# Two buffers for gathered token rows, and one slot's preparation moved by one place

## The chip, the cores and the metric

The kernel runs on one core of a Trainium2 chip. The metric is the device time of one execution in microseconds (us), taken over several runs. The engines of the core are TensorE (PE in the profile; PEld is its weight load), VectorE (DVE), ScalarE (ACT), GpSimd (POOL) and SyncE (SP), which here only issues DMAs.

## The reference

Banded attention is followed by a mixture of experts with one expert per token.

```python
# attention: 8 batches, 8 heads, 576 positions, 64 columns a head
mask_plain = (rel >= 0) & (rel < 32)                       # heads 0-3
mask_dil = (rel >= 0) & (rel < 128) & (rel % 4 == 0)       # heads 4-7
scores = np.where(masks, (q @ k.T) / 8, -1e9)
attn = softmax(scores);  x = (attn @ v) as [4608, 512]
# experts: 8, with 512 -> 1024 -> 512
logits = x @ w_gate + modality_bias[modality_id]
e_idx = argmax(logits);  gate_w = softmax(logits)[e_idx]
for e in range(8):
    mask = e_idx == e
    out[mask] = gate_w[mask, None] * (relu(x[mask] @ w1[e]) @ w2[e])
```

All inputs and outputs are float32.

## The kernel before

**Attention.** The work is cut into 72 units (9 for each batch). In the main loop (L1160) each turn does one stage of several units: `scores` (L420: products of q and k, the mask added by DVE, the row maximum, and the subtraction `sm` on POOL), `exp` on ACT, `probsT`, `attend`, `normalize`, and then the store of x into DRAM (`x_dram`, two halves) and the gate's logits. Products into `pss` (one buffer) for the next unit can start when DVE has read the last ones.

**Constants.** The generator `constants` (L239) is advanced beside the first turns. It sets up tables for the routing: POOL sets the buffer `xr` to zero (L251), fills `sent`, and makes index ramps (`pay`, `place`, `ewt_i`, `eoff_i`); DVE turns these into float tables (L281 to L294). DVE's instructions stand in the order of the code, so that its steps for the constants stand ahead of the mask addition of the unit that follows.

**Routing.** `gating` (L556) works out each token's expert and its place in a table in DRAM, and writes the tokens' numbers there by scatters from POOL (L619, six a batch). Groups of 256 tokens of one expert are called slots. The first four slots are taken after three batches, so that the experts' work can begin before attention has ended. There are 19 slots in the static part (the last holds 128 tokens), numbered from 0; "the third slot" is slot 2.

**A slot's rows.** The rows take this way:
- `fetch_ids` (L757): SP loads the token numbers `idt` of the slot.
- `gather` (L766): POOL fetches the rows with four indirect DMAs into the SBUF buffer `xr` (L775); SP writes `xr` to `x_slot` in DRAM (L780), and, when the slot before has been read (`taken`), loads it back as `xg` in another layout with four DMAs (L786). `xr` has one buffer, which one memset in `constants` has set to zero, since a row whose number is out of bounds is not written.
- `prepare_x` (L926): for each half of 128 tokens DVE transposes blocks of `xg` into `xt` (L937), ACT casts `xt` to the rounded part `xh` (L943), and DVE subtracts for the rest `xl` (L946). The four steps are: transpose of half 0; cast and subtraction of half 0; transpose of half 1; cast and subtraction of half 1.

**A slot's products.** `slots` (L971) does for each slot eight columns of work, f = 0 to 7, called places here. At each place PE makes twelve products of w1 and x into `ph` (L1071): for each of four blocks of rows `w1h * xh`, `w1h * xl` and `w1l * xh`. Then ACT and DVE make `hh` and `hl` (L1077, L1078) from the result, and PE makes the six second products (L989) of an earlier place. After them stand `split_w2` of this place and `split_w1` for the place after the next one; a split is a cast on ACT (L955) and a subtraction on DVE (L956). At the end of a slot ACT scales the result into `ys` (L992) and POOL scatters it to the output.

**What sets the order.** `ahead(n, f, end)` (L1096) is called twice at each place of slot n. It asks for weight loads, token numbers and gathers of later slots, one step a call. At the end of a place (`end`) it also does one step of `prepare_x` for slot n + 1, from a place on that the condition in L1116 gives. PE, DVE, ACT and SP keep the order of the code; POOL's order is set when the program is built, but most of its instructions (those by way of `pool`, among them gathers, memsets, output scatters) keep the order of the code among themselves. Each engine works through its queue in order, SP's DMA issues included.

Of the kernel before, what the change touches and what calls it, by code (L numbers as in the profile page):

```python
# [10 lines left out]
F32 = mybir.dt.float32  # L11
# [13 lines left out]
DM = H * D  # L25
# [33 lines left out]
def kernel(  # L59
# [13 lines left out]
    P = 128  # L73
# [4 lines left out]
    gat = ctx.enter_context(tc.tile_pool(name="gat", bufs=2))  # L78
# [160 lines left out]
    def constants():  # L239

        yield
        nc.scalar.copy(out=wgs[:, :, 0:NE], in_=wg)
        yield
        mid_t = spare[1][0:B, 0:S]
        for i in range(2):
            for a in range(2):
                nc.vector.tensor_copy(out=mid_t.rearrange("b (a c i j) -> b a i c j", a=2, c=2, i=2)[:, a, i],
                                      in_=mid[i][:, :, 0].rearrange("b (j c a) -> b a c j", c=2, a=2)[:, a])
            yield
        yield  # L250
        pool.memset(gat.tile([P, 2, DM], F32, name="xr", bufs=1), 0.0)  # L251
        sent = spare[1][:, S:S + (NE + 1) * NT * 3 // P].bitcast(I32)
        pool.memset(sent, SENT)
        yield
        pm = psum['o'].tile([P, 512], F32, name="po")
        for c in range(NGB):
            nc.tensor.transpose(out=pm[0:GB, B * c:B * (c + 1)], in_=mid_t[:, GB * c:GB * (c + 1)], identity=ident[:B, :B])
        mid_f = cpool.tile([GB, NBLK], F32, name="mid_f")
        nc.vector.tensor_copy(out=mid_f.rearrange("p (b c) -> p c b", c=NGB), in_=pm[0:GB, 0:NBLK].rearrange("p (c b) -> p c b", b=B))
        yield  # L260
        mid_n = cpool.tile([GB, NBLK], F32, name="mid_n")
        nc.vector.tensor_scalar(out=mid_n, in0=mid_f, scalar1=-1.0, scalar2=1.0, op0=ALU.mult, op1=ALU.add)
        mtmp = cpool.tile([GB, NE, NBLK], F32, name="mtmp")
        nc.gpsimd.tensor_tensor(out=mterm, in0=mid_n.rearrange("p (o c) -> p o c", o=1).broadcast_to([GB, NE, NBLK]),
                                in1=bias_sb[:, 0, :].rearrange("p (e o) -> p e o", o=1).broadcast_to([GB, NE, NBLK]), op=ALU.mult)
        nc.gpsimd.tensor_tensor(out=mtmp, in0=mid_f.rearrange("p (o c) -> p o c", o=1).broadcast_to([GB, NE, NBLK]),
                                in1=bias_sb[:, 1, :].rearrange("p (e o) -> p e o", o=1).broadcast_to([GB, NE, NBLK]), op=ALU.mult)
        nc.gpsimd.tensor_tensor(out=mterm, in0=mterm, in1=mtmp, op=ALU.add)
        yield
        nc.sync.dma_start(out=table.rearrange("(p a) t -> p (a t)", p=P), in_=sent)  # L270

        pool.iota(pay[:, :, 2], pattern=[[GB, NBLK]], base=0, channel_multiplier=1)
        place = cpool.tile([GB, 2, NBLK], I32, name="place")
        pool.iota(place[:, 0], pattern=[[0, B], [GB, NGB]], base=0, channel_multiplier=1)
        pool.iota(place[:, 1], pattern=[[S, B], [0, NGB]], base=0, channel_multiplier=0)
        ewt_i = cpool.tile([GB, NE, NGB], I32, name="ewt_i")
        pool.iota(ewt_i, pattern=[[-1, NE], [0, NGB]], base=NE, channel_multiplier=0)
        eoff_i = cpool.tile([GB, NE, NGB], I32, name="eoff_i")
        pool.iota(eoff_i, pattern=[[NT, NE], [0, NGB]], base=0, channel_multiplier=0)
        yield  # L280
        nc.vector.tensor_copy(out=ewt, in_=ewt_i)  # L281
        nc.vector.tensor_copy(out=eoff, in_=eoff_i)
        pool.memset(ones_bf, 1.0)
        pool.affine_select(out=upper, in_=ones_bf, pattern=[[1, GB]], compare_op=ALU.is_gt,
                                fill=0.0, base=0, channel_multiplier=-1)
        for t in x_dram:
            nc.sync.dma_start(out=t[NT:NT + 1, :], in_=zero)
        placef = cpool.tile([GB, 2, NBLK], F32, name="placef")
        nc.vector.tensor_copy(out=placef, in_=place)
        past = cpool.tile([GB, NBLK], F32, name="past")  # L290
        nc.vector.tensor_scalar(out=placef[:, 1], in0=placef[:, 0], scalar1=float(NCLS), scalar2=None, op0=ALU.mult)
        for r in range(1, NCLS):
            nc.vector.tensor_scalar(out=past, in0=placef[:, 0], scalar1=float(CL * r), scalar2=float(NCLS * CL - (2, -1, 2)[r - 1]), op0=ALU.is_ge, op1=ALU.mult)
            nc.vector.tensor_tensor(out=placef[:, 1], in0=placef[:, 1], in1=past, op=ALU.subtract)  # L294
        yield
        nc.vector.tensor_copy(out=place[:, 0], in_=placef[:, 1])
        nc.vector.tensor_tensor(out=pay[:, :, 0], in0=place[:, 0], in1=place[:, 1], op=ALU.add)
        yield
        nc.vector.tensor_copy(out=sidx[:, :, 0], in_=sidx_i)
# [22 lines left out]
    pool = InOrder()  # L322
# [443 lines left out]
    def gather(n, ids):  # L766


        idt, nu = ids
        xr = gat.tile([P, 2, DM], F32, name="xr", bufs=1)  # L770
        nrows = round_rows(n)
        queue = nc.sync
        for u in range(nu):
            for kd in range(2):
                pool.indirect_dma_start(out=xr[:, u, 256 * kd:256 * kd + 256], out_offset=None, in_=x_dram[kd][0:nrows, :],  # L775
                                        in_offset=bass.IndirectOffsetOnAxis(ap=idt[:, u, 2 * kd:2 * kd + 1], axis=0),
                                        bounds_check=nrows - 1, oob_is_err=False)
                yield
        yield
        queue.dma_start(out=x_slot[0:P * nu, :].rearrange("(u p) c -> p u c", p=P), in_=xr[:, 0:nu])  # L780
        yield
        while 0 < n < NS and n - 1 not in taken:
            yield
        xg = gat.tile([P, 2 * KC, P], F32, name="xg", bufs=1)
        for r in range(KC):
            queue.dma_start(out=xg[BLK * r:BLK * (r + 1), 0:nu * KC],  # L786
                              in_=x_slot[0:P * nu, P * r:P * (r + 1)].rearrange("(g i) c -> i g c", i=BLK))
        state['xg', n] = xg
# [30 lines left out]
    def round_rows(n):  # L819

        for (b, _), r0 in zip(EARLY, round_from[1:]):
            if n < r0:
                return (b + 1) * S
        return NT + 1
# [15 lines left out]
    def load_more(n, pieces):  # L840

        if n not in loads_of and n in si_of:
            loads_of[n] = [fetch_weights(si_of[n], n == 0), 0]
        if n in loads_of:
            for _ in range(min(pieces, 6 - loads_of[n][1])):
                next(loads_of[n][0], None)
                loads_of[n][1] += 1
# [119 lines left out]
    def split_w2(g):  # L967
        f = g % FC
        w2p[g] = split(w2q[f // 2][:, f % 2, :], [P, DM], "w2")

    def slots(ns, ids_of, ahead, hold=lambda n, f: (), base=0):  # L971


# [122 lines left out]
    def ahead(n, f, end):  # L1096

        if not end:
            todo['calls'] += 1
            load_more(n, 2)  # L1100
            i = todo['ids']
            if i < NS and i <= n + 3 and fetch_slot(i):
                todo['ids'] += 1
                born[i] = todo['calls']
            i = todo['rows']
            if not fetching and i < NS and i <= n + 2 and i in ids_of and todo['calls'] > born.get(i, -2) + 1:
                fetching.append((i, gather(i, ids_of[i])))
                todo['rows'] += 1
        if fetching and (not end or fetching[0][0] <= n + 1):
            if next(fetching[0][1], fetching) is fetching:  # L1110
                fetching.pop(0)
        if n + 1 == NS or not end or n + 1 not in ids_of:
            return
        due = sum(f >= x for x in (1, 2, 3, 5, 6, 7))
        load_more(n + 1, min(2, due - (loads_of[n + 1][1] if n + 1 in loads_of else 0)))
        if f >= (3 if n + 1 < 4 else 2):  # L1116
            if n + 1 not in preparing:
                preparing[n + 1] = prepare_x(n + 1, ids_of[n + 1])
            next(preparing[n + 1], None)
# [7 lines left out]

    units, turned = [], []
    tasks = [(-1, constants())]
    moe = None  # L1130
    man = ExitStack()
# [109 lines left out]
    with tc.For_i(NSTAT, NSTAT + left, 1) as i:  # L1241
        si = slot_regs(state['info', len(EARLY)], i)
        ids = fetch_ids(si)
        run(gather(NS, ids), fetch_weights(si, False), prepare_x(NS, ids), slots(1, [ids], lambda n, f, end: None, base=NS))
# [29 lines left out]
```

## Time and profile before

| | |
|---|---|
| median of 3 runs | 672.0 us (671.12 to 672.9) |
| profiled execution | 671.78 us |
| its span, first to last instruction | 670.0 us |
| mean granted TensorE clock | 0.989 |
| POOL's gathers (`xr<-x_dram`) | 74, median 1056 ns each |
| memset of `xr` | 1, 961 ns |
| transposes of `prepare_x` (L937) | 37, median 705 ns |

A row of a timeline reads: start, duration, engine, line, operation, output<-inputs, shapes, count, and in brackets the idle time of the engine before it with what ended that. A row of waits reads: who waited, for whom, us in total, times, the longest. "issue" is a wait for nothing that the profile shows. A granted clock of 1.00 is TensorE's full speed.

### The profile page before, as it was taken

The numbers are of one execution on the slowest core, as the hardware profiler recorded it, in microseconds if no ns is written. First come the engines' busy times: TensorE is split into PE (matmuls) and PEld (weight loads), VectorE is DVE, ScalarE is ACT, GpSimd is POOL, SyncE is SP. The second block draws the span as 40 slices with busy tenths as digits, with TensorE's granted clock in tenths as the row PEclk, the third lists the DMA queues.
The fourth block names the chain that finished last, engine by engine and source line by source line (L and its number), as shares of the span: only waits on it lengthen the run. The fifth ranks groups of instructions, "written<-read, shape, count | busy, mean of one in ns | idle before, by whom it ended". The sixth has DMA issues, their size and how long they took to land. (4 is left out here: it accounts for less than half of the span.)

```text
span 670.0 us, 17986 instructions
## 1 busy us (share of the span) xinstructions
PE 639.5 (95%) x6394; PEld 553.0 (83%) x6396; DVE 487.9 (73%) x1204; ACT 418.6 (62%) x897; POOL 258.6 (39%) x322
## 2 busy tenths in 40 slices
PE   8899999999998979999999999999999999999994
PEld 4788788778776868799989999899999999999972
DVE  6788888887789547977587668667776777677653
ACT  4677877877776345556566656665666566656663
POOL 5634665657766425333332232232413231321101
PEclk9999999999999789999999999999999999999998
DMA  9989899879879624976952338723312335931470
GB/s 196 222 203 213 188 195 211 156 181 203 194 164 246 181 45 99 230 167 181 256 172 72 88 95 258 183 80 111 123 68 79 111 117 128 274 97 64 109 185 24
DMA packets 133408, 103.33 MB, mean 154 GB/s; under 512 B 67424, under 2 KB 111474, under 8 KB 133316
## 3 DMA queue, kind: packets, MB, share of 16 engines
q1 hardware_dynamic: 124724, 82.30, 51.9%
q0 software_dynamic: 8176, 19.26, 9.8%
q8 instruction: 51, 0.84, 0.6%
q10 hardware_dynamic: 416, 0.59, 0.3%
q14 instruction: 41, 0.34, 0.2%
HBM read 127.52 MB, written 29.39 MB: 234 GB/s over the span
## 5 line engine op out<-in xcount | busy, mean ns | idle before, releaser
L1071 PE MATMUL pt<-xh,w1l 128*128 128x256 f32 x576 | 163.7, 284 | 2.1 <-DVE w1l L956 1.1
L1071 PE MATMUL pt<-xh,w1h 128*128 128x256 f32 x576 | 164.7, 286 | 0.9 <-issue 0.9
L1071 PE MATMUL pt<-xl,w1h 128*128 128x256 f32 x576 | 163.2, 283 | 1.6 <-DVE xl L946 1.6
L1077 ACT ACTIVATE hh<-pt 128x256 fp32r<-128x256 f32 x144 | 55.2, 383 | 151.8 <-PE pt L1071 144.1
L956 DVE TENSOR_TENSOR w2l<-w2q,w2h 128x512 fp32r<-128x512 f32 x152 | 104.5, 689 | 38.8 <-ACT w2h L955 24.8
L314 POOL DMA_INDIRECT xr<-x_dram,idt x74 | 82.2, 1111 | 112.6 <-DMA x_slot<-xr 69.0
L1071 PEld LDWEIGHTS pt<-xh,w1h 128*128 128x128 f32 x576 | 109.9, 191 | 9.4 <-issue 3.0
L314 POOL DMA_INDIRECT out_dram<-ys,idt x37 | 41.5, 1121 | 197.0 <-ACT ys L992 124.4
L1078 DVE SCALAR_TENSOR_TENSOR hl<-pt,hh 128x256 fp32r<-128x256 f32 x144 | 60.6, 421 | 76.4 <-ACT hh L1077 66.4
L1071 PEld LDWEIGHTS pt<-xl,w1h 128*128 128x128 f32 x576 | 109.8, 191 | 7.5 <-DVE xl L946 1.9
L989 PE MATMUL py<-w2h,hh 128*128 128x512 f32 x288 | 115.3, 400 | 0.0
L989 PE MATMUL py<-w2h,hl 128*128 128x512 f32 x288 | 114.0, 396 | 0.0
L989 PE MATMUL py<-w2l,hh 128*128 128x512 f32 x288 | 112.6, 391 | 0.0
L1071 PEld LDWEIGHTS pt<-xh,w1l 128*128 128x128 f32 x576 | 110.2, 191 | 2.4 <-DVE w1l L956 1.8
L956 DVE TENSOR_TENSOR w1l<-w1q,w1h 128x512 fp32r<-128x512 f32 x152 | 103.7, 684 | 6.4 <-ACT w1h L955 3.4
L955 ACT CAST w1h<-w1q 128x512 fp32r<-128x512 f32 x152 | 94.2, 622 | 5.9 <-PE py L989 3.1
L955 ACT CAST w2h<-w2q 128x512 fp32r<-128x512 f32 x152 | 93.0, 613 | 0.4 <-PE py L989 0.4
L314 POOL TENSOR_TENSOR sm<-sm,nmx 128x384 f32<-128x384 f32 x72 | 65.1, 904 | 71.8 <-DVE den L459 40.6
L445 ACT COPY pT<-pt 96x512 f32<-96x512 f32 x72 | 41.6, 578 | 46.4 <-PE pt L442 24.8
L989 PEld LDWEIGHTS py<-w2l,hh 128*128 128x128 f32 x288 | 54.4, 189 | 13.4
L452 PE MATMUL po<-vw,pT 96*64 96x65 f32 (+1 forms) x1216 | 54.0, 227 | 8.9 <-issue 3.1
L989 PEld LDWEIGHTS py<-w2h,hh 128*128 128x128 f32 x288 | 54.9, 191 | 6.9
(196 smaller groups left out, 1018.5 us busy)
## 6 DMA issues: line engine op xcount, KB each, us to landing
w2q<-in_moe_w_dram SPq DMA_DIRECT2D x76, 512.0 KB
w1q<-in_moe_w_dram SPq DMA_DIRECT2D x152, 256.0 KB
x_slot<-xr SPq DMA_DIRECT2D x18, 512.0 KB
xg<-x_slot SPq DMA_DIRECT2D x72, 128.0 KB
x_dram<-x_sb SPq DMA_DIRECT2D x32, 256.0 KB
st<-in_q_dram SPq DMA_DIRECT2D x32, 144.0 KB
st<-in_k_dram SPq DMA_DIRECT2D x32, 144.0 KB
vw<-in_v_dram SPq DMA_DIRECT2D x16, 288.0 KB
```

The costliest lines, as they stand in the source:

```text
L314: ins = tc.keep_in_program_order(getattr(nc.gpsimd, name)(*args, **kw))
L445: nc.scalar.copy(out=self.pT, in_=src)
L452: nc.tensor.matmul(out=pov[r0:r0 + nr, g, cs], lhsT=self.pT[:, 2 * g + a, r0:r0 + nr], rhs=self.vts[kd][:, blk, cs], start=True, stop=True)
L955: nc.scalar.copy(out=hi, in_=raw)
L956: nc.vector.tensor_tensor(out=lo, in0=raw, in1=hi.bitcast(F32), op=ALU.subtract)
L989: nc.tensor.matmul(out=py[u], lhsT=ht[:, us], rhs=wt, start=(f + n == 0), stop=(f + n == FC + 1))
L1071: nc.tensor.matmul(out=ph, lhsT=wt[:, c, :], rhs=xt[:, c, 0:cols], start=(c + i == 0), stop=(c + i == KC + 1))
L1077: nc.scalar.activation(out=hh, in_=ph, func=AF.Relu)
L1078: nc.vector.scalar_tensor_tensor(out=hl, in0=ph, scalar=0.0, in1=hh.bitcast(F32), op0=ALU.max, op1=ALU.subtract)
```

## The change

Three edits. `constants` sets two buffers to zero, with a second memset of the same size on POOL. `gather` takes its `xr` from two buffers in turn, so that a gather waits only for the x_slot write of the slot before the last one. And the condition for `prepare_x` gives place 3 as the first for slots 1 and 3 alone; slot 2 begins at place 2 of slot 1, as the slots from 4 on did already.

```diff
-        pool.memset(gat.tile([P, 2, DM], F32, name="xr", bufs=1), 0.0)
+        for _ in range(2):
+            pool.memset(gat.tile([P, 2, DM], F32, name="xr", bufs=2), 0.0)
...
-        xr = gat.tile([P, 2, DM], F32, name="xr", bufs=1)
+        xr = gat.tile([P, 2, DM], F32, name="xr", bufs=2)
...
-        if f >= (3 if n + 1 < 4 else 2):
+        if f >= (3 if n + 1 in (1, 3) else 2):
```

## The prediction

> **What bounds the kernel now.** I read the page first, then the busy time of the engines by stretches, then the waits of POOL and PE, and last the timelines of PE, DVE, POOL and SP around the places that the edits touch. The page:
>
> ```profile
> span 670.0 us, 17986 instructions
> PE 639.5 (95%) x6394; PEld 553.0 (83%) x6396; DVE 487.9 (73%) x1204; ACT 418.6 (62%) x897; POOL 258.6 (39%) x322
> ```
>
> TensorE is busy for 95% and POOL, whose waits the first edit is about, for 39%. An average over three stages says little, so here are seven stretches of the same execution (bounds, length, then busy time and count for PE, PEld, DVE, ACT, POOL, then granted clock, DMA share, GB/s):
>
> ```profile
> 0.00:30.00 30.00, 25.02 (x322) 16.93 (x325) 20.46 (x70) 16.89 (x39) 18.23 (x49) 1.00 1.09 198
> 30.00:215.00 185.00, 178.63 (x3275) 148.18 (x3274) 155.41 (x523) 141.07 (x324) 109.60 (x153) 1.00 0.89 197
> 227.00:241.00 14.00, 10.46 (x99) 8.10 (x98) 5.00 (x16) 4.53 (x10) 10.15 (x10) 1.00 0.48 95
> 241.00:246.00 5.00, 4.48 (x16) 2.98 (x16) 3.22 (x9) 2.14 (x5) 0.00 (x0) 0.66 0.13 43
> 256.00:262.00 6.00, 6.00 (x44) 5.46 (x43) 5.20 (x16) 2.58 (x6) 5.08 (x4) 1.00 0.43 114
> 262.00:290.00 28.00, 26.40 (x171) 23.48 (x171) 22.93 (x78) 16.73 (x35) 11.36 (x10) 1.00 0.93 194
> 290.00:650.00 360.00, 359.44 (x2280) 324.01 (x2278) 252.80 (x444) 215.81 (x444) 98.22 (x90) 1.00 0.48 137
> ```
>
> From 290 to 650 us, most of the mixture of experts, PE lacks only 360.00 - 359.44 = 0.56 us. Nothing that shortens a wait of another engine there can give more than that. What PE can still win lies before 290: 28.00 - 26.40 = 1.60 us between 262 and 290, and 3.54 + 0.52 = 4.06 us between 227 and 246, where the granted clock of the last 5 us is 0.66 as well.
>
> **The two gather buffers, at POOL.** The wait that they remove, and where it is longest:
>
> ```profile
> POOL xr L314 <- DMA x_slot<-xr: 69.0, 13, 15.3
> ...
> 227.06 1.46 POOL L314 DMA_INDIRECT xr<-x_dram,idt  x1 [6.28 <-DMA x_slot<-xr]
> 229.59 0.95 POOL L619 DMA_INDIRECT table<-pay,dst  x1 [1.07 <-DVE pay L610]
> ...
> 239.80 0.92 POOL L619 DMA_INDIRECT table<-pay,dst  x1 [0.30 <-issue]
> 256.01 1.47 POOL L314 DMA_INDIRECT xr<-x_dram,idt  x1 [15.29 <-DMA x_slot<-xr]
> ```
>
> ```profile
> 252.40 0.38 SPq L780 DMA_DIRECT2D x_slot<-xr  x1
> ```
>
> Thirteen gathers start late by 69.0 us in all, because the write of the rows to x_slot still reads the only buffer. With two, the first gather of slot 2 can start 6.28 us sooner, near 220.8, and slot 3's four 15.29 us sooner, near 240.7. Who gains from that? After the gather comes the x_slot write, on SP's queue. For slot 2 it was issued at 252.40, 11.7 us after POOL's block with its gathers had ended (239.80 + 0.92), so it waited for its turn on SP and not for the rows. Behind POOL's waiting gathers stand table scatters, whose inputs come from DVE (the one at 229.59 waits for pay), and the out scatters, which wait for ACT. I find no step of PE that waits for a gather, directly or through SP: I cost the removed wait at 0. The cover for that is PE's own work, and if it were gone, at most the 0.56 us of the late stretch and the 4.06 us of 227 to 246 could move; the second is a rival below. What is moved past: on POOL the gathers overtake nothing in the order of the code, only time; on SP no order changes.
>
> **The second memset.** It costs one more memset of the size of this one, on POOL, in the opening:
>
> ```profile
> 16.81 0.96 POOL L314 MEMSET xr<- 128x1024 f32 x1
> 17.70 0.92 POOL L314 MEMSET w1q<- 128x972 int32 x1
> ...
> 19.96 0.83 POOL L266 TENSOR_TENSOR mtmp<-mid_f,bias_sb 96x384 f32<-96x384 f32 x1 [0.28 <-DVE mid_f L259]
> ...
> 23.93 0.19 POOL L314 IOTA ewt_i<- 96x48 int32 x1
> ```
>
> ```profile
> 24.15 0.28 DVE L281 CAST ewt<-ewt_i 96x48 f32<-96x48 int32 x1 [0.82 <-POOL ewt_i L314]
> ...
> 25.98 0.55 DVE L429 TENSOR_TENSOR sm<-pss,masks 128x384 f32<-128x384 f32 x1
> ```
>
> ```profile
> 26.58 0.56 PE L427 MATMUL pss<-kT,qT 64*64 64x96 f32 x16 [0.34 <-DVE sm L429]
> ```
>
> Start to start the memset takes 17.70 - 16.81 = 0.89 us. POOL has 0.28 us of idle time at 19.96 and then works on without a listed wait up to ewt_i, so that iota comes 0.89 - 0.28 = 0.6 us late. DVE waits for it (0.82 us), has its chain of small steps and the mask addition at 25.98 behind it, and PE waits for that addition before its scores at 26.58. This chain has no slack shown in it, and the stretch behind it, 30 to 215, is one in which PE is busy for 178.63 of 185.00 us: 0.6 us of delay goes through to the end. Its bounds are 0, if a later PE wait of the attention stage swallows it, and the full 0.89. I take +0.6, since three waits in a row name the next link.
>
> **The third slot's rows one place sooner.** In slot 1, prepare_x of slot 2 now runs at places 2, 3, 4, 5 and not 3, 4, 5, 6. It issues two transposes and two subtractions on DVE and two casts on ACT, no DMA. Setting taken(2) one place earlier (4, not 5) frees nothing: slot 3's xg loads are asked for one step per place and reach that test only at place 7. The gain is at the change of slots:
>
> ```profile
> 280.09 0.28 PE L1071 MATMUL pt<-xh,w1h 128*128 128x256 f32 x1
> 281.97 0.39 PE L1071 MATMUL pt<-xl,w1h 128*128 128x256 f32 x1 [1.60 <-DVE xl L946]
> 282.19 0.28 PE L1071 MATMUL pt<-xh,w1l 128*128 128x256 f32 x1
> ...
> 285.01 0.35 PE L1071 MATMUL pt<-xh,w1l 128*128 128x256 f32 x1
> ```
>
> ```profile
> 277.06 0.70 DVE L937 STREAM_TRANSPOSE xt<-xg 128x512 f32<-128x512 f32 x1
> ...
> 280.04 0.67 DVE L956 TENSOR_TENSOR w2l<-w2q,w2h 128x512 fp32r<-128x512 f32 x1
> 280.64 0.67 DVE L956 TENSOR_TENSOR w1l<-w1q,w1h 128x512 fp32r<-128x512 f32 x1
> 281.24 0.67 DVE L946 TENSOR_TENSOR xl<-xt,xh 128x512 fp32r<-128x512 f32 x1
> ...
> 284.24 0.67 DVE L956 TENSOR_TENSOR w1l<-w1q,w1h 128x512 fp32r<-128x512 f32 x1
> ```
>
> PE's second product of slot 2 waits 1.60 us for the last subtraction, at 281.24. One place sooner, that subtraction (0.67 us) takes the slot of the transpose (0.70 us) at 277.06, so everything up to 280.64 on DVE stays where it is. But the third product needs w1l, and that runs on DVE from 280.64 to 281.31. So the wait does not go: its releaser becomes w1l. The third product then starts 0.06 us after 281.31 (as the second did after 281.24 + 0.67 = 281.91), at 281.37 and not 282.19. The product after it follows by 0.22 us, as after the first wait, so some 0.7 us are won. The next w1l, at 284.24, shifts by the 0.6 us that DVE no longer spends before it, and PE needed it at 285.01, 0.10 us after its end: 0.6 us is what stays. The bounds are 0 and 0.72. What of the new place 2?
>
> ```profile
> 266.49 0.68 DVE L956 TENSOR_TENSOR w1l<-w1q,w1h 128x512 fp32r<-128x512 f32 x1
> 267.60 0.42 DVE L1078 SCALAR_TENSOR_TENSOR hl<-pt,hh 128x256 fp32r<-128x256 f32 x1 [0.44 <-ACT hh L1077]
> ```
>
> ```profile
> 259.11 1.84 SPq L786 DMA_DIRECT2D xg<-x_slot  x4
> ```
>
> ```profile
> 263.53 0.95 POOL L619 DMA_INDIRECT table<-pay,dst  x1 [1.50 <-DMA xg<-x_slot]
> ```
>
> The first transpose would start at about 267.1. Its data was asked for at 259.11 and had landed by 263.53 in part, and I see nothing that would hold the rest for 3.5 us more. DVE has 0.44 us of idle time before 267.60, so hl comes about 0.2 us late, and it is not PE's next need. ACT has room for two casts: it waits for PE before nearly every hh.
>
> ```profile
> ACT hh L1077 <- PE pt L1071: 144.1, 117, 2.8
> ```
>
> **The sum.** -0.6 (change of slots) + 0.6 (opening) + 0 (buffers) = 0. The profiled execution took 671.78 us, a span of 670.0 and 1.78 around it; the median of the three runs is 672.0. With a sum of 0 I predict that median, **672.0**. On bounds alone this case lies between 672.0 - 0.7 = 671.3 and 672.0 + 0.9 = 672.9.
>
> **A rule against the row.** The Trainium skill (Trainium Kernel Development and Optimization, Best Practices) says to double-buffer so that DMA and compute overlap. By it the 69.0 us would be worth something; the row of 290 to 650 leaves 0.56 us for it to win there, so the trace does not agree for this stage, and only the second stall, 227 to 246, could make it right.
>
> **The rivals.** One is a gain in that stall. PE loses 4.06 us there, and the clock of 0.66 over 5 us means (1 - 0.66) x 5.00 = 1.7 us more. The longest single wait names no releaser:
>
> ```profile
> 236.05 0.69 PE L452 MATMUL po<-vw,pT 96*64 96x65 f32 x16 [2.24 <-issue]
> ```
>
> It coincides with POOL's densest block, ten DMAs from 227.06 to 240.72, gathers and scatters in turn. If these are what holds PE, and the free buffer lets the gathers of slot 2 go before 229.59 into the 6.28 us in which POOL now waits, the block ends some 3 us sooner. Then at least the last 0.52 us and the 1.7 us of slow clock go (-2.2), at most all (-5.8). I take the 1.7 and nearly half of the 4.06, -3.5: **668.5**. For it: nothing else shown accounts for the 2.24 us. Against it: in 256 to 262 POOL issues four gathers back to back and PE is busy for 6.00 of 6.00 us.
>
> The other is a loss at the same place. Slot 3's four gathers, 5.08 us of POOL (256 to 262), now follow the ten without a break, from 240.7 to about 246. If POOL's DMAs hold PE at the rate of 227 to 241 (3.54 us idle in 10.15 us of POOL), that is 5.08 x 3.54 / 10.15 = 1.8 us, and a second stretch of slow clock adds 1.7: +3.5, **675.5**. It decides if PE shows idle time without a releaser after 242. For: the slow clock shows that PE is weak there anyway. Against: again the 6.00 of 6.00.
>
> The Trainium skill (TensorE: Matmul & The Clock Gate, Part 1) has the clock halved only after an idle window of about 3.4 us; by that rule the 1.8 us alone would not slow it and the loss would be 673.8. The 0.66 here followed idle times of 2.24 us and less, so the row does not bear the rule out as it stands, and I keep the 1.7.
>
> Last, one of the two small terms may be absent: the opening hidden and 0.6 won (671.4), or xl or w1l no sooner and the memset paid in full (672.9).
>
> **Chances.** The forecast 0.48, the gain in the stall 0.25, the loss in it 0.15, one term absent 0.12. A measurement of this kernel can tell about 0.3% from no change, 2.0 us: under 670.0 is faster, 0.25; over 674.0 is slower, 0.15; between, 0.48 + 0.12 = 0.60. The range takes in the loss and more than half of the gain's span, **668.0 to 675.5**; the forecast's own is 671.3 to 672.9.
>
> **What would show it.** Right: no wait of POOL's gathers on x_slot of the size of 15.29; the wait of 1.60 at the change to slot 2 shrunk to about 1 with w1l as releaser; PE's scores near 26.58 later by 0.6; PE from 290 to 650 as before. Wrong: the idle time from 227 to 246 far from 4.06 us in either direction, a granted clock there other than 0.66, scores at 26.58 unmoved, or a wait on xg at place 2.

## The result, and the profile after

The changed kernel took 681.68 us (median of 6 runs, 678.03 to 684.16) beside 672.45 for the kernel before (6 runs, 670.66 to 677.67). The ratio is 1.0133, 95% interval [1.0099, 1.0167]: slower by some 9 us. (A ratio leaves disturbed executions out, so it is not always the quotient of the medians given with it.) The profiled execution took 682.84 us, its span is 681.1.

The page of the changed kernel (its line numbers are one higher from its second memset on), then four of the seven stretches (bounds, length, busy time and count for PE, PEld, DVE, ACT, POOL, then granted clock, DMA share, GB/s):

```profile
span 681.1 us, 17960 instructions
PE 647.5 (95%) x6394; PEld 557.3 (82%) x6396; DVE 484.0 (71%) x1204; ACT 419.4 (62%) x897; POOL 259.1 (38%) x323
```

```profile
0.00:30.00 30.00, 25.33 (x262) 17.29 (x268) 18.35 (x62) 13.79 (x31) 18.47 (x49) 0.83 1.11 196
227.00:241.00 14.00, 10.21 (x105) 8.43 (x102) 6.22 (x21) 4.74 (x11) 8.62 (x9) 0.87 0.56 102
241.00:246.00 5.00, 3.77 (x17) 2.34 (x15) 0.42 (x1) 1.41 (x3) 3.78 (x5) 0.67 0.28 30
290.00:650.00 360.00, 357.65 (x2269) 321.70 (x2268) 248.54 (x454) 214.91 (x441) 100.50 (x90) 1.00 0.47 136
```

The shares of the page say nothing. The stretches do: the first 30 us ran at a clock of 0.83, PE is idle for 3.79 + 1.23 = 5.02 us of 227 to 246 where it was for 4.06, and after 290 it now lacks 360.00 - 357.65 = 2.35 us where it lacked 0.56.

The trace of each kernel has 6394 products of PE, and all but one of them pair up in the same order, so the start of one can be set against the start of its twin. Where the changed kernel loses or wins, in us, between the same products (times are those of the kernel before):

| stretch | before | changed | difference |
|---|---|---|---|
| to 30 | 30.0 | 33.2 | +3.2 |
| 30 to 227 | 197.0 | 195.4 | -1.6 |
| 227 to 252 | 25.0 | 31.6 | +6.5 |
| 279 to 290, change to slot 2 | 10.8 | 10.0 | -0.8 |
| 300 to 330 | 30.0 | 33.8 | +3.9 |
| the rest | | | +0.1 |

The sum, +11.3, is the difference of the spans within 0.2. Two places carry most of it: the stretch of the second rival, and one that no part of the prediction names. The same PE work of 227 to 252, with its bounds in each execution, first before and then changed:

```profile
227.00:252.00 25.00, 20.95 (x155) 16.22 (x154) 12.99 (x34) 9.70 (x22) 10.15 (x10) 0.93 0.30 64
```

```profile
228.58:260.10 31.52, 24.25 (x155) 18.34 (x154) 13.13 (x35) 9.76 (x22) 13.07 (x14) 0.78 0.35 67
```

155 product records in each. PE is idle for 31.52 - 24.25 = 7.27 us, not 25.00 - 20.95 = 4.05, and its clock is 0.78, not 0.93. POOL has 14 instructions there and not 10: its block of gathers and scatters, and behind it slot 3's four gathers without a pause. The timelines of POOL and PE in the changed kernel:

```profile
227.79 1.05 POOL L315 DMA_INDIRECT xr<-x_dram,idt  x1 [3.13 <-issue]
...
241.54 0.92 POOL L620 DMA_INDIRECT table<-pay,dst  x1 [0.30 <-issue]
242.77 1.03 POOL L315 DMA_INDIRECT xr<-x_dram,idt  x1 [0.30 <-issue]
...
246.76 1.01 POOL L315 DMA_INDIRECT xr<-x_dram,idt  x1 [0.30 <-issue]
```

```profile
239.20 1.14 PE L453 MATMUL po<-vw,pT 96*64 96x65 f32 x16 [3.79 <-issue]
245.62 0.32 PE L507 MATMUL pt<-ident,x_sb 128*128 128x128 f32 x1 [1.14 <-issue]
247.04 0.28 PE L1072 MATMUL pt<-xh,w1l 128*128 128x256 f32 x1 [0.86 <-issue]
...
249.88 0.78 PE L990 MATMUL py<-w2h,hh 128*128 128x512 f32 x1 [0.34 <-issue]
```

PE's waits without a releaser begin in POOL's block and go on until 249.88, 2 us after its last gather.

The second place is quieter. POOL's timeline, before and changed:

```profile
300.77 1.00 POOL L314 DMA_INDIRECT xr<-x_dram,idt  x1 [0.30 <-issue]
307.26 1.46 POOL L314 DMA_INDIRECT xr<-x_dram,idt  x1 [5.49 <-DMA x_slot<-xr]
...
312.95 1.03 POOL L314 DMA_INDIRECT out_dram<-ys,idt  x1 [0.30 <-issue]
319.83 1.00 POOL L314 DMA_INDIRECT out_dram<-ys,idt  x1 [5.85 <-DMA out_dram<-ys,idt]
328.70 1.06 POOL L314 DMA_INDIRECT xr<-x_dram,idt  x1 [7.87 <-DMA x_slot<-xr]
```

```profile
303.54 1.17 POOL L315 DMA_INDIRECT xr<-x_dram,idt  x1 [0.43 <-issue]
...
313.62 1.00 POOL L315 DMA_INDIRECT xr<-x_dram,idt  x1 [0.30 <-issue]
320.36 1.01 POOL L315 DMA_INDIRECT xr<-x_dram,idt  x1 [5.73 <-DMA idt<-table]
...
325.78 1.04 POOL L315 DMA_INDIRECT out_dram<-ys,idt  x1 [0.30 <-issue]
```

Before, a wait of 5.49 parts slot 4's four gathers from slot 5's, and two output scatters stand ahead of slot 6's (328.70). Changed, eight gathers run from 303.54 to 314.62, and slot 6's four come ahead of both scatters: the second buffer also let the program's builder put POOL's instructions into another order. ACT in the same microseconds:

```profile
306.42 0.39 ACT L1078 ACTIVATE hh<-pt 128x256 fp32r<-128x256 f32 x1 [2.32 <-PE py L990]
310.22 0.39 ACT L1078 ACTIVATE hh<-pt 128x256 fp32r<-128x256 f32 x1 [2.38 <-PE py L990]
315.38 0.39 ACT L1078 ACTIVATE hh<-pt 128x256 fp32r<-128x256 f32 x1 [3.23 <-PE pt L1072]
```

```profile
307.47 0.28 PE L1072 MATMUL pt<-xh,w1l 128*128 128x256 f32 x1
...
313.10 0.39 PE L1072 MATMUL pt<-xl,w1h 128*128 128x256 f32 x1 [0.51 <-DVE xl L947]
316.84 0.38 PE L1072 MATMUL pt<-xh,w1h 128*128 128x256 f32 x1 [0.78 <-ACT w1h L956]
```

The hh at 310.22 waits for a semaphore of PE alone (a semaphore is the counter by which one engine tells another that it is done). The last of its twelve products ended at 307.47 + 0.28 = 307.75, and ACT had been idle for 2.38 us: the signal is 2.4 us late. The casts of weights behind hh on ACT are late with it, and at 316.84 PE waits for one. This lateness can be counted: for each hh after 255 us before which ACT had been idle for over 0.2 us, the start of hh less the end of its last product, counted up to ACT's idle time. With no indirect DMA of POOL beside it, the start follows after 0.04 us, and 1 of 71 is late by over 0.3 (the changed kernel). With one beside it, 21 of 37 are, by up to 3.23. In the kernel before it is 6 of 50, by up to 1.24. A late hh need not cost time: 16 of the 21 come after 345 us, and from 330 to 650 PE's time grew by 0.1 us only.

So the theory (**free gathers**; the expectations of e1 to e8 call it the theory of bursts): PE's completion signals come late while POOL issues one indirect DMA after another; the wait for the only buffer had parted them, and without it runs grow long enough for the lateness to reach PE. Its rivals: the **opening** (the second memset makes the 3.2), the **place** (the third edit), and the **second buffer** itself.

### The profile page after: what moved, and what is told of

Read it like the earlier page. It is cut to its first block, busy times and chain, and to the rows that moved or that the text cites. A ratio compares the mean times of both kernels' runs of the same rounds, so it can differ in the third digit from the quotient of the medians.

```text
span 681.1 us, 17960 instructions
## 1 busy us (share of the span) xinstructions
PE 647.5 (95%) x6394; PEld 557.3 (82%) x6396; DVE 484.0 (71%) x1204; ACT 419.4 (62%) x897; POOL 259.1 (38%) x323
## 5 line engine op out<-in xcount | busy, mean ns | idle before, releaser
L315 POOL DMA_INDIRECT out_dram<-ys,idt x37 | 39.9, 1079 | 252.7 <-ACT ys L993 213.4
L990 PEld LDWEIGHTS py<-w2l,hh 128*128 128x128 f32 x288 | 54.5, 189 | 13.5
L453 PE MATMUL po<-vw,pT 96*64 96x65 f32 (+1 forms) x1216 | 55.9, 231 | 8.9 <-issue 5.1
L453 PEld LDWEIGHTS po<-vw,pT 96*64 96x64 f32 (+1 forms) x1216 | 44.9, 138 | 20.6 <-ACT pT L446 6.3
```

Source lines behind the costliest of these rows:

```text
L315: ins = tc.keep_in_program_order(getattr(nc.gpsimd, name)(*args, **kw))
L453: nc.tensor.matmul(out=pov[r0:r0 + nr, g, cs], lhsT=self.pT[:, 2 * g + a, r0:r0 + nr], rhs=self.vts[kd][:, blk, cs], start=True, stop=True)
L990: nc.tensor.matmul(out=py[u], lhsT=ht[:, us], rhs=wt, start=(f + n == 0), stop=(f + n == FC + 1))
```

## The experiments

The kernels ran on four chips as they came: A (the first eight), B (four), C (two), D (four); which of them, or another, the result's was is not known. Each is compared with the kernel before on the same chip, whose median was 672.2 and 674.5 on A, 663.2 on B, 673.1 on C, 674.4 on D.

(Where a count is blank, none was taken. e11, one run on B, stands in its section alone.)

| kernel | chip | us | ratio [95%] | late hh beside POOL |
|---|---|---|---|---|
| e1 third edit alone | A | 670.69 | 1.0001 [0.9964, 1.0038] | 3 of 48 |
| e2 two buffers alone | A | 679.42 | 1.012 [1.0068, 1.0171] | 21 of 39 |
| e3 memset twice, one buffer | A | 673.75 | 1.0019 [0.9985, 1.0053] | |
| e4 changed, first gather paced | A | 678.64 | 1.0102 [1.0063, 1.0141] | 21 of 39 |
| e5 before, order of the code | A | 682.97 | 1.0124 [1.0082, 1.0167] | 1 of 43 |
| e6 changed, order of the code | A | 680.8 | 1.009 [1.0058, 1.0122] | |
| e7 gathers doubled | A | 694.9 | 1.0294 [1.0221, 1.0367] | 9 of 71 |
| e8 doubled, apart | A | 721.12 | 1.071 [1.0641, 1.078] | 2 of 56 |
| e9 changed, all paced | B | 662.88 | 0.999 [0.996, 1.0019] | 0 of 46 |
| e10 changed, slot 3 paced | B | 663.97 | 1.0009 [0.9975, 1.0044] | 0 of 36 |
| e12 changed | B | 662.84 | 1.0003 [0.9973, 1.0033] | 0 of 38 |
| e13 changed, all paced | C | 673.35 | 1.001 [0.9974, 1.0047] | 3 of 48 |
| e14 changed, no weight loads | C | 674.02, once | | 4 of 44 |
| e15 changed, slot 3 paced | D | 678.38 | 1.0042 [0.9999, 1.0085] | |
| e16 changed | D | 681.52 | 1.0127 [1.0066, 1.0189] | 20 of 37 |
| e17 changed, chained | D | 690.1 | 1.0266 [1.0212, 1.0319] | 0 of 46 |
| e18 before | D | 674.53 | 1.0034 [0.9991, 1.0077] | 6 of 48 |

e18 is the kernel before against itself: 0.34% is what this comparison makes of nothing.

**One part alone (e1, e2, e3).**

```diff
e1: -        if f >= (3 if n + 1 < 4 else 2):
    +        if f >= (3 if n + 1 in (1, 3) else 2):
e2: the first two edits of the change
e3: +        xr0 = gat.tile([P, 2, DM], F32, name="xr", bufs=1)
    +        for _ in range(2):
    +            pool.memset(xr0, 0.0)
```

> The kernel before with the third edit alone (rows of the third slot one place sooner). Theory of bursts (the loss comes from gathers that no longer wait for the x_slot write and so leave POOL in long unbroken runs): 671.9, 0.6 under the kernel before, with the wait of 1.60 at the change to slot 2 cut to about 0.7 and 227 to 250 as before. Theory of the opening (the second memset costs the most): the same 671.9. Theory of the place (the sooner transposes disturb DVE while the table is written): some 2 us slower, lost between 262 and 290.

> The kernel before with the first two edits alone (two buffers, two memsets). Theory of bursts: 682.3, as slow as the changed kernel plus the 0.6 of the third edit, with PE idle in 239 to 250 and in 312 to 318. Theory of the place: 673, since the edit that hurts is gone.

> The kernel before with its one buffer set to zero twice, so that only POOL's 0.9 us in the opening is added. Theory of bursts: 673.0 (between 0 and +0.9 over the kernel before), PE at 30 us late by 0.6. Theory of the opening: 676, PE at 30 us late by 3.7 with a stretch of half clock between 20 and 30.

The two buffers alone make the loss (1.012); the place does not (1.0001), and neither does the memset (1.0019, with 1 in the interval). The opening falls as a rival. PE reaches the product of 30 us 0.4 to 1.4 us late in five further profiles with one memset (e18, the kernel before itself, is the latest), and 0.4 to 1.2 late in twelve with two. The +3.2 of the changed kernel's first profile and +2.3 in that of e2 come with a clock of 0.54 and 0.73 in 20 to 30; e16, the same program as the first, has +0.7 and a clock of 1.00 there.

**Pacing one gather (e4).** Its wait was put on the first gather of each slot:

```diff
+                if u + kd == 0 and 'rows_out' in state:
+                    wait_all(ins.ins, [state['rows_out']])
```

> The changed kernel, all three edits, but the first gather of each slot also waits for the x_slot write of the slot before, so that the gathers are paced as with one buffer while the second buffer, its address and its memset stay. Theory of bursts: 672.5, near the kernel before, no idle PE in 312 to 318, 4 us in 227 to 250. Theory of the opening: 676 or so, the opening's 3.7 stays. If two buffers hurt by where they lie in SBUF: 681.

1.0102. It did not test what it was meant to: the builder moved the waiting gather behind the other three, which ran freely (241.9, 243.3, 244.6, then 259.8). It is the case of three free gathers of four, and costs nearly as much as four.

**The order of the code, and more gathers (e5 to e8).** POOL's order forced to that of the code by dropping `and 'go' not in state` where `pool` records an instruction; e7 and e8 add four gathers a slot from slot 6 on:

```diff
e7: +            xd = gat.tile([P, 2, DM], F32, name="xd", bufs=1)
    +            ... four gathers into xd, behind those into xr
e8: +            ... four gathers into xr, behind the x_slot write
```

> The kernel before, one buffer, with POOL's order forced to the order of the code to the end (before, this holds only until the experts start, and the program's builder puts the gathers of slots 4 and 5 next to each other). Theory of bursts: 672, because with one buffer the x_slot wait already parts the gathers of one slot from those of the next, and the block at 227 to 241 stays as it is; its change is within 1.5. It is the base for the two kernels with doubled gathers.

> The changed kernel, all three edits with both buffers free to be used, and only POOL's order forced to the order of the code, so that twelve gathers of slots 4 to 6 no longer stand in a row and slot 3's four stand between the table scatters of the last batch. Theory of bursts: 672, no idle PE in 312 to 318, 227 to 250 as in the kernel before. Rival (the second buffer hurts by itself, or gathers that start sooner hurt wherever they are): 679 to 682, as the changed kernel.

> The kernel before with POOL's order as in the code, and from slot 6 on four more gathers of the same rows, into a buffer that nobody reads, right behind a slot's gathers without a wait: twelve bursts of eight and one of four. Theory of bursts: each of the twelve holds hh of ACT by 1 to 3 us several times and costs PE 0.3 to 2.8 us as the burst at 303 of the changed kernel and of the two-buffer kernel did; 690 (675.6 to 706). Rival (the amount gathered counts, not the bursts): slower by the same as the kernel with the gathers apart. Rival (gathers don't hold PE at all): 672.

> As the kernel with doubled gathers, the same number of bytes and of indirect DMAs, but the four more gathers go into the slot's own buffer and so wait until the x_slot write has read it: bursts of four with some 5 us between. Theory of bursts: 673 (672 to 676), hh late by more than 1 us rarely. Rival (amount): as slow as the doubled kernel.

None went the way expected: e7's time lies in the theory's range and e6's in the rival's, but the traces show other reasons. In the order of the code slot 3's gathers stand between the last batch's scatters (272.5 to 280.4 in e5), so its rows come late, and at the change to slot 3 the one-buffer kernel loses 6.6 us:

```profile
294.09 0.58 PE L1071 MATMUL pt<-xh,w1h 128*128 128x256 f32 x1 [3.24 <-ACT w1h L955]
```

Against that base the second buffer costs nothing (e6 1.009, e5 1.0124). e7's twelve runs of up to eight gathers made only 9 of 71 hh late, and PE's time from 345 to 600 grew by 2.5 us over e5, not by 3.6 to 34 (another 6.9 us over the kernel before are lost after 650): a run's length alone does not decide. e8 is slower still, but by another way, so it says nothing of amount against runs: SP waits for rows to land before each x_slot write (142.2 us in all from 285 on, against 64.8 in e5), the weight loads queue behind it, and PE waits 24.6 us for w1h.

**The changed kernel on a chip without late signals (e9 to e12).**

```diff
e9:  +                if n > 0:
     +                    wait_all(ins.ins, [state['rows_out']])
e10: the same with n == 3
e11: +        if n > 3:
     +            if n in si_of:
     +                loads_of[n] = [None, 6]
     +            return
```

> The changed kernel with its second buffer and both memsets, but all four gathers of a slot (not the first alone) wait for the x_slot write of the slot before; POOL's order becomes again that of the kernel before. Theory of free gathers (the loss is what the removed wait had kept apart): 672.5, 0 to 0.9 over the kernel before, PE's loss in 227 to 250 and in 303 to 330 as before, hh late by over 0.3 in about 6 of 40 places with a POOL DMA beside them (before 6 of 41, changed 19 of 33). Rival (the second buffer, its address or its memset hurts by itself): 679 to 682.

> The changed kernel, but the four gathers of slot 3 alone wait for the x_slot write of slot 2; the later slots are free, in the changed kernel's order. Theory of free gathers: the block at 227 to 241 ends as before and 4 to 6 of the loss are regained, the idle PE of 303 to 330 stays: 676. Rival (all of the loss is made after 290 or in the opening): 680 to 682. If 227 to 250 holds all of it: 672.

> The changed kernel without the weight loads from slot 4 on (left out of the computation: those slots use the last weights), so that SP issues few DMAs beside POOL's gathers while these keep their order. If hh is late because POOL's indirect DMAs and SP's issues come together: hh late by over 0.3 in at most 3 of some 37 places with POOL beside them, and no idle PE from 303 to 330. If POOL's run of gathers alone does it: about half of them late, as in the changed kernel (21 of 37), and PE idle there by 2 to 4.

> The changed kernel again, for a second profile. Theory of free gathers: PE loses again 5 to 7 us more than the kernel before in 227 to 250 and 1.5 to 4 in 303 to 330; the half clock of the opening (3 us in the first profile) belongs to chance and need not come again, since the kernel with two memsets in one buffer was late by 0.3 at 30 us. Rival (the opening is caused by the second memset): again late by some 3 us at 30 us.

On B no expectation could be told from another: the kernel before takes 663.2 and the changed one 662.84, and no hh was late, in any of the four kernels (e11, one run, 661.28). The same run of eight gathers is there in e12, from 289.97 to 300.95, and ACT does not notice it:

```profile
293.74 0.38 ACT L1078 ACTIVATE hh<-pt 128x256 fp32r<-128x256 f32 x1 [1.40 <-PE pt L1072]
296.55 0.38 ACT L1078 ACTIVATE hh<-pt 128x256 fp32r<-128x256 f32 x1 [0.88 <-PE pt L1072]
299.37 0.38 ACT L1078 ACTIVATE hh<-pt 128x256 fp32r<-128x256 f32 x1 [1.40 <-PE pt L1072]
302.18 0.38 ACT L1078 ACTIVATE hh<-pt 128x256 fp32r<-128x256 f32 x1 [1.40 <-PE pt L1072]
```

One hh every 2.81 us. The work of 227 to 252, 155 product records and a dense POOL, takes 18.5 us with no gap at full clock (18.5 or 18.6 in all four):

```profile
227.60:246.10 18.50, 18.50 (x155) 14.93 (x153) 13.10 (x35) 9.68 (x22) 13.62 (x13) 1.00 0.52 95
```

So the kernel before, too, loses 25.0 - 18.5 = 6.5 us there on its chip. A signal is late in it as well: the last transpose of `pe`, which makes the `pt` that ACT copies to `pT`, ends on PE at 232.19, and the copy, for which ACT has been idle, starts at 235.42.

**Pacing where signals are late (e13 to e16).**

> The changed kernel with all four gathers of a slot waiting for the x_slot write of the slot before, once more, since the last four kernels ran on a chip where no signal of PE was late in any of them. If the kernel before shows 670 to 675 here (a chip with late signals): by the theory of free gathers 672 to 675, ratio to the kernel before under 1.005, and few hh late; by the rival (the second buffer or its memset itself) a ratio of 1.010 to 1.013 as for the changed kernel. If the kernel before shows 660 to 664: ratio 1.000 and no hh late, by either.

> The changed kernel without the weight loads from slot 4 on (left out of the computation), once more. On a chip with late signals: if SP's issues are needed for the lateness, hh late by over 0.3 in at most 3 of some 40 places with POOL beside them; if POOL's run of gathers alone makes it, in about half of them. On a chip without: in none.

> The changed kernel, slot 3's four gathers alone waiting for the x_slot write of slot 2, once more. On a chip where the kernel before shows 670 to 675 (late signals): if the free gathers of slot 3 make most of the loss, 674 to 677, between the kernel before and the changed kernel, and PE's loss in 227 to 250 as before; if the run of gathers after 290 makes it, 680 to 682. On a chip where it shows 660 to 664: no difference.

> The changed kernel, for its time on the same chip as the two beside it. Late signals: 680 to 682, ratio 1.010 to 1.013. No late signals: ratio 1.000.

With the wait given back to all gathers, and the second buffer and its memset still there, the time is that of the kernel before (1.001, on C), where the changed kernel is at 1.0133 in the result and at 1.0127 on D, all with late signals. The changed kernel itself did not run on C, so that it would have lost as much there is taken over from the others and not shown. The second buffer as such is cleared by this and by e12, where it is there too and costs nothing (1.0003, on B). With slot 3 alone paced it is 1.0042 [0.9999, 1.0085], between the kernel before and the changed one, but the interval overlaps that of e16: how much of the loss hangs on slot 3's four gathers and how much on the later slots stays open.

The trace of e13 warns against placing the loss by one execution. Slot 3's gathers do wait in it, until 257.68, and yet the work of 227 to 252 takes 29.8 us, not 25.0; 30 to 227 is 3.8 shorter than in the kernel before. Nearly all of PE's idle time is one wait for `pT` within POOL's block of ten:

```profile
223.90:253.70 29.80, 21.02 (x156) 16.84 (x153) 13.24 (x35) 9.71 (x22) 10.10 (x10) 0.83 0.27 56
```

```profile
237.89 0.92 POOL L620 DMA_INDIRECT table<-pay,dst  x1 [0.30 <-issue]
238.86 0.58 ACT L446 COPY pT<-pt 96x512 f32<-96x512 f32 x1 [12.28 <-remote]
239.49 1.14 PE L453 MATMUL po<-vw,pT 96*64 96x65 f32 x16 [8.78 <-ACT pT L446]
```

The products that this copy needs had ended at 229.10; it starts 0.05 us after POOL's last scatter ends. So the block, which stands in both kernels, can by itself cost more than the 7.27 us of PE's idle time in the changed kernel. Taken together, 30 to 252 lasts 222.0 us in the kernel before, 221.2 in e18, 220.0 in e1 and 223.0 in e13, but 226.9 in the changed kernel, 226.2 in e2, 228.9 in e16 and 226.4 in e14, whose gathers are free: the loss shows there, but not the split by place within it.

e14 shows three late hh among its twelve gathers and one besides; PE's 300 to 330 takes 29.9, as in the kernel before. Without SP's weight loads lateness seems rarer, but no kernel with free gathers and weight loads ran on chip C, so SP's part stays open.

**Never two in flight (e17, and e18 beside it).**

```diff
gather, and the table scatters of the last batch but one:
+                if 'ind' in state:
+                    wait_all(ins.ins, [state['ind']])
+                state['ind'] = ins.ins
```

> The changed kernel with both buffers free, but each gather (and each table scatter of the last batch but one) also waits until the gather or such scatter before it has landed, so that POOL never has two of these in flight. If signals are late because POOL's indirect DMAs pile up in flight: hardly any hh late by over 0.3 (at most 3 of some 40 places with POOL beside), and 668 to 674 where the changed kernel takes 681. If it is enough that POOL issues one after another: late as in the changed kernel, 680 to 683.

> The kernel before, for a second profile beside the other three on the same chip. On a chip with late signals PE loses in 227 to 250 again about 4 us and hh is late by over 0.3 in some 6 of 41 places with POOL beside; on a chip without, in none, and the whole time is near 663.

The lateness is gone: 0 of 46, where the changed kernel on the same chip shows 20 of 37. The work of 227 to 252 takes what it takes on B, first e17 and then e16:

```profile
240.10:258.60 18.50, 18.50 (x155) 14.92 (x153) 13.00 (x34) 9.69 (x22) 5.31 (x5) 1.00 0.14 44
```

```profile
227.60:259.60 32.00, 24.65 (x155) 18.58 (x154) 13.21 (x35) 9.86 (x22) 13.82 (x14) 0.73 0.35 71
```

13.5 us won, and more given back elsewhere, as POOL now waits for landings with other work queued behind it: 9.5 us in 30 to 215 (one wait of PE is 4.50 us for DVE's `sm`, while POOL's own step on `sm` stands behind a gather that waits 5.37 us), and 7.1 at the change to slot 2, where PE waits 7.0 us for `ys`, and ACT ahead of that for the landing of an output scatter. So 690, not the 668 to 674 expected, with the lateness gone as expected. The chain also sets POOL's DMAs further apart in time (5 and not 14 in this work), so it does not tell whether the number in flight or the pause between issues is what counts.

## Why the prediction was wrong

- **The two buffers at POOL, 0: the step that failed.** It asked which step of PE waits for a gather, found none, and cost the removed wait at 0. It did not ask what the wait kept apart: POOL's indirect DMAs, beside which signals of PE come late. Measured in place of the 0: 1.2% for the two buffers alone (e2), 1.3% for the change (the result and e16), some 8 us; with the wait given back 0.1% (e13, on another chip).
- **The first gather "near 220.8".** It came at 227.79, after 3.13 us for which the profile names no releaser. Less the 1.6 us by which PE's work is late there, that is 226.2: under 1 us sooner than 227.06, not 6.28. Another wait stood behind the one named; the gather waits for several semaphores, and which came last is not shown. Slot 3's four came at 242.77, as worked out (240.7 and the delay).
- **"The gathers overtake nothing in the order of the code."** The builder's order changed: slot 6's gathers went ahead of two output scatters. Twelve gathers with no scatter between them follow from that.
- **The rival of a loss in the stall** had the mechanism, and its sign (idle time without a releaser after 242) is there. Its price was +3.5 and its chance 0.15; the stretch lost +6.5, of which 7.27 - 4.05 = 3.2 is idle time and 24.25 - 20.95 = 3.3 longer products at the slower clock (one execution of each; e13 above shows how far that stretch moves by itself). The signs that it named lay in 227 to 246, where idle time and clock, 5.02 us and 0.67 from 241 on, stayed near the 4.06 and 0.66; the rest of the loss came behind. Against the rival stood "again the 6.00 of 6.00" of 256 to 262, a single run of four gathers with the wait ahead of it: the very case in which the wait did its work. That a run after 290 could be late as well (+3.9 in the first profile, +1.7 in e16, +1.5 in e2) stood in no case of the prediction.
- **The rival of a gain in the stall** did not come about: the block did not end sooner, since the first gather did not start sooner. Nor does a closer block help by itself: in e13 the pause of 1.07 is gone from it, and PE's idle time is 8.78 us.
- **The second memset, +0.6**: not to be seen (e3 1.0019; the spread of like kernels at 30 us is over 1 us).
- **The place, -0.6**: right, in mechanism and nearly in size. The wait became one for w1l, and 279 to 290 is shorter by 0.8 (0.9 in e1, e9 and e12). In e16 the last batch's scatters fell on it and it lost 2.4 instead.

```profile
289.22 0.39 PE L1072 MATMUL pt<-xh,w1l 128*128 128x256 f32 x1 [0.64 <-DVE w1l L957]
```

On chip B, then, "no change" was the answer (1.0003); in the result and on D it was not. The prediction's steps were those of a chip on which signals are never late, though the 2.24 us without a releaser had been seen.

## What to carry to other kernels

A wait that nobody downstream needs may still be doing a job: before costing its removal at 0, look at what will then run without a pause, and whether idle times without a releaser already coincide with such runs. When a kernel's second buffer is for indirect DMAs, count how many can then follow one another without a pause, and look at the new order of that queue, not at the wait alone. And take the base and the change to more than one chip when the disputed cost is a wait that the profile can't name.

## What the runs showed of the hardware

- Signals of PE come late beside POOL's indirect DMAs: by up to 3.2 us in the changed kernel, while without such a DMA 0.04 us is usual. It was gone where each gather waits for the landing of the one before (e17: 0 of 46), and it depends on the chip: on B 0 late of 120 in e9, e10 and e12 together, with the same programs. In the block of e13 one came 9.8 us late (229.10 to 238.86), but in e7 runs of up to eight gathers made only 9 of 71 late: what makes it strong stays open. The profile models the ends of products, so it can't tell a late signal from a late end, though PE had gone on to its next products meanwhile. Why the chips differ, and what in the chip holds the signal, no run here shows.
- On B, where no signal is late, the kernel before is faster by 9 us or more (663.2 against 672.2 to 674.5), as much as the change cost elsewhere.
- The clock of TensorE fell to half after short idle times. Stretches of 2 us in the changed kernel's opening:

```profile
16.00:18.00 2.00, 1.30 (x26) 1.10 (x26) 0.00 (x0) 1.11 (x3) 1.97 (x3) 1.00 1.35 214
18.00:20.00 2.00, 2.00 (x31) 1.88 (x28) 1.72 (x5) 0.56 (x2) 2.00 (x3) 0.74 0.90 160
20.00:22.00 2.00, 1.41 (x11) 1.11 (x11) 0.82 (x4) 1.69 (x4) 1.72 (x3) 0.50 0.98 252
```

```profile
16.70 0.53 PE L352 MATMUL pt<-ident,st 96*128 96x96 f32 x4 [1.09 <-DMA st<-in_k_dram]
```

No single wait of PE from 6 us on was longer than this 1.09 before the clock fell to 0.50. The Trainium skill (TensorE: Matmul & The Clock Gate, Part 1) has it halved only after an idle window of about 3.4 us; if idle means that PE makes no product at all, these rows do not agree.
